# A first-layer token block moves to seven products, its weight values go through DRAM, and one block's token values change engine

## The chip, the cores and the metric

The kernel runs on one core of one Trainium2 chip, as one launch. The metric is the device time of a run in microseconds (us). Five engines work side by side, each through its own instructions in order: TensorE (PE in the profile), VectorE (DVE), ScalarE (ACT), GpSimd (POOL) and SyncE (SP), which here only issues DMA transfers.

## The reference

Clustered attention feeds two dense layers, all in float32. The change touches only the two layers and the last steps of attention beside which the first layer starts.

```python
attn_out = _attn_ref(q, k, v, centroids)              # 2 batches, 8 heads, 768 tokens, head size 64
x = attn_out.transpose(0, 2, 1, 3).reshape(1536, 512)
...
h = x @ w_in                                          # first layer: 512 -> 2048
x = (np.maximum(h, 0) + np.log1p(np.exp(-np.abs(h)))) @ w_out   # 2048 -> 512
...
h = x @ w_in2                                         # second layer, same sizes
out = (h * np.clip(h + 3.0, 0.0, 6.0) / 6.0) @ w_out2
```

The four weight matrices arrive as float64. The kernel reads them as pairs of 32-bit words and builds float32 values from the bits.

## The kernel before

**Steps.** The 1536 tokens are cut into three blocks of 512 (block 0, 1, 2), the 2048 hidden columns into 16 pieces of 128 (f = 0 to 15). One step n = (layer, block, f) forms the hidden values of one piece for one block (`phase_a`, 12 matmuls of 512 columns), passes them through the layer's function (`hid_scalar`, `hid_gate`, `hid_hi`, `hid_lo`), and adds their product with `w_out` to the block's four output banks y0 to y3 (`phase_b`, 12 matmuls of 512 columns; `back` issues them LAG = 2 steps later). There are 12 matmuls and not 4 because each float32 operand is kept as a rounded part and a rest (`xhi`/`xlo` for tokens, `pi`/`po` for weights, `ghi`/`glo` for hidden values) and three of the four partial products are computed. The first layer is n = 0 to 47, the second n = 48 to 95.

**Conversion.** In block 0 of the first layer the pieces of the weights are converted while they are used: piece f in step f - 2, both its `w_in` part (tiles `ri`, `pi`) and its `w_out` part (`ro`, `po`). `convert_abs` is a ScalarE copy (L123) into a tile `val`, `convert_bits` three VectorE operations on it (L131, L133, L137, in this order), `convert_parts` a ScalarE copy that rounds (L147), `convert_rest` a subtraction (L158, in this block on VectorE). The tiles `val` come from a pool of four buffers in the layers, two per step; in attention the pool has one. The copies for step n + 1 are made at the end of step n. Conversion of the second layer's pieces is spread over later steps.

**Fetching.** Pieces 7 to 15 of the first layer are fetched by 18 transfers of 512 KB (`fetch_w`, L103), which stand on SP's queue right behind the transfers of the last attention step (`row`, and `rsb`, which spreads the softmax sums). Transfers count their completion on eight semaphores in turn, DMAHW0 to DMAHW7, and one that is about to count on a semaphore first waits for the transfer that counted there before it.

**Pairs.** In the second layer, blocks 1 and 2 run two steps at a time by Strassen's scheme. The 2x2 cut is: two hidden pieces (f, f + 1), two halves of the 512 input columns, two halves of the block's tokens. Seven products (`product`, L1054, six matmuls of 256 columns each) take the place of eight. Four of them need sums of weights (`factor_totals` on VectorE, `factor_part` on ScalarE and GpSimd) and sums of tokens (`token_sums`), which stand in the columns of `xhi` and `xlo` that held the block before (`token_parts`). The sums of weights are made from the float32 values of `w_in`. So `keep_values` stores each second-layer `val` of `w_in` to DRAM when its third bit operation is done (L971), and `factor_fetch` brings it back (L980).

**Ends of blocks.** `finish_block` empties y0 to y3 when a block's last `phase_b` is done: ScalarE writes the rounded part into `xhi` (L922), VectorE the rest into `xlo` (L923). For block 2 ScalarE also copies each bank to a tile `tok` (L927), from which the token sums of the second layer's block 2 are made.

Of the kernel before, what the change touches and what calls it, by code (L numbers as in the profile page):

```python
# [22 lines left out]
def cluster_attention_then_two_mlps(  # L23
# [30 lines left out]
    def f32(ap):  # L54
        return ap.bitcast(F32)
# [114 lines left out]
    steps = [(l, tb, f) for l in range(2) for tb in range(NB) for f in range(NF)]  # L170
    ps_h = []
    hs = {}
    last_flip = []

# [12 lines left out]
    def attention():  # L187
        with ExitStack() as st, ExitStack() as st_ld, ExitStack() as st_ps:
# [514 lines left out]
            at(94, 2, convert_bits, *piece, 2)  # L703
            at(94, 3, convert_parts, *piece, False)
# [165 lines left out]
    spill = ctx.enter_context(tc.tile_pool(name="spill", bufs=1, space=bass.MemoryType.DRAM))  # L870
# [25 lines left out]
    def hidden(layer, h, paired=False):  # L896
        t = {"h": h, "layer": layer}
        t["ghi"] = tmp.tile([P, TB], F32R, tag="ghi", name="ghi")
        t["glo"] = tmp.tile([P, TB], F32R, tag="glo", name="glo")
        if layer == 1:  # L900
# [62 lines left out]
    fac, tok, part, kept = {}, {}, {}, {}  # L963
    A, Bp = slice(0, TB // 4), slice(TB // 4, TB // 2)
    near, far = slice(0, NC // 2), slice(NC // 2, NC)

    def keep_values(layer, f, nm):

        if layer == 1 and nm == "i":
            kept[f] = spill.tile([P, NC, P], F32, tag=f"v{f}", name=f"v{f}")  # L970
            nc.sync.dma_start(kept[f], pieces[layer, f, nm][1])  # L971

    def factor_fetch(n):

        layer, tb, f = steps[n]
        if tb == 1:
            fac[n] = []
            for e in range(2):
                v = wpools["val"].tile([P, NC, P], F32, tag="val", name="wv")
                nc.sync.dma_start(v, kept[f + e])  # L980
# [15 lines left out]
    def factor_part(n, e):  # L996
        if n in fac:
            w = part[n, e] = win.tile([P, 2, NC, P], F32R, tag=f"s{e}", name=f"s{e}")
            nc.scalar.activation(w[:, 0], fac[n][e], AF.Copy)
            nc.gpsimd.tensor_tensor(w[:, 1], fac[n][e], f32(w[:, 0]), ALU.subtract)  # L1000
            f = steps[n][2]
# [3 lines left out]
    def token_values(c):  # L1005
        cols = slice(TB, 2 * TB)
        x = tok[1, c] = win.tile([P, 2, TB], F32, tag=f"x{c}", name=f"x{c}")
        for e in range(2):
            k = c + 2 * e
            nc.gpsimd.tensor_tensor(x[:, e], f32(xhi[k][:, cols]), f32(xlo[k][:, cols]), ALU.add)  # L1010

    def token_sums(tb, c, step):
# [7 lines left out]
        nc.gpsimd.tensor_tensor(o, p, q, ALU.subtract)  # L1020
# [45 lines left out]
    with tc.manual_schedule():  # L1066
        gs, ysd = {}, {}
        late = None
# [27 lines left out]
        for n in range(first_pair):  # L1096
# [19 lines left out]
            if (NB - 1) * NF + LAG < n <= (NB - 1) * NF + LAG + 4:  # L1116
                k = n - (NB - 1) * NF - LAG - 1
                if k % 2 == 0:
                    token_values(k // 2)
                for m in range(k % 2 * 2, k % 2 * 2 + 2):  # L1120
                    token_sums(1, k // 2, m)
            k = n - NB * NF - LAG - 1
            if 0 <= k < 8:
                token_sums(2, k // 4, k % 4)
                if k % 4 == 3:
                    token_store(2, k // 4)
# [31 lines left out]
        order = [(first_pair - 2, None, None), (first_pair - 1, None, None)]  # L1158
        for n in range(first_pair, len(steps), 2):
            f = steps[n][2]  # L1160
            order += [(n, f == 0, False), (n + 1, False, f == NF - 2)]

        def backs():
            for what in order:
                yield from back(*what)

        chunks = backs()
        for n in range(first_pair, len(steps), 2):
            layer, tb, f = steps[n]
            more = n + 2 < len(steps)  # L1170
            change = f == NF - 2 and tb + 1 < NB
# [8 lines left out]
            if tb + 1 < NB and f == 6:  # L1180
# [39 lines left out]
        for _ in chunks:  # L1220
            pass
# [47 lines left out]
```

## Time and profile before

| | |
|---|---|
| median of 3 runs (lowest to highest) | 749.52 us (749.39 to 750.17) |
| the profiled execution, its own time | 749.33 us |
| its span in the profile | 747.6 us |
| granted TensorE clock over the span | 1.00 of full |
| TensorE / VectorE / ScalarE / GpSimd busy | 724.9 / 538.4 / 441.9 / 200.3 us |

The span runs from the first to the last recorded instruction. The difference to the execution's time lies around it. Attention fills the span up to about 249 us, the first layer from there to about 506 us (block 0 until about 338, block 1 until about 420), the second layer the rest. Times of single rows are starts, counted from the start of the span.

### The profile page before, as it was taken

What the parts mean: (1) busy time and instruction counts of PE and PEld (TensorE: products, weight loads), DVE (VectorE), ACT (ScalarE), POOL (GpSimd) and SP (SyncE); (2) the same over time, 40 slices, a digit from 0 to 9 for tenths busy, and PEclk for the clock granted to TensorE, in tenths of its full rate; (3) what the DMA queues carried; (4) which work ended last, traced back from release to release, by engine and by line L of the source; (5) the groups of instructions that cost most, each with busy time, mean ns of one, the idle gap of its engine ahead of it and who ended that gap; (6) DMA issues with size and microseconds to landing.
All of it is one profiled execution on the core that took longest, in us unless ns stands there. A gap on an engine that the chain in (4) does not pass through costs nothing.

```text
span 747.6 us, 11713 instructions
## 1 busy us (share of the span) xinstructions
PE 724.9 (97%) x4129; PEld 642.3 (86%) x4129; DVE 538.4 (72%) x932; ACT 441.9 (59%) x859; POOL 200.3 (27%) x267
## 2 busy tenths in 40 slices
PE   7999999999999899999999999998999999999997
PEld 6788899898888788788888888886888999999997
DVE  5999889889898999942111258887996888765553
ACT  6889889889998856632212346565565444533322
POOL 3667768767435000000000410003002422410000
PEclk9999999999999999999999999999999999999999
DMA  7656776666474490000000267771114364235311
GB/s 197 176 142 171 171 199 178 164 186 163 111 194 152 164 363 1 2 0 1 1 0 1 71 209 246 236 236 45 71 57 155 142 226 169 115 137 200 113 57 57
DMA packets 50410, 98.66 MB, mean 132 GB/s; under 512 B 5904, under 2 KB 26800, under 8 KB 50352
## 3 DMA queue, kind: packets, MB, share of 16 engines
q1 hardware_dynamic: 50208, 97.79, 42.4%
q8 instruction: 32, 0.52, 0.3%
q14 instruction: 26, 0.21, 0.1%
q10 hardware_dynamic: 144, 0.13, 0.1%
HBM read 59.93 MB, written 16.83 MB: 103 GB/s over the span
## 4 chain that ended last, share of the span: by engine, by line
PE 69%; DVE 18%; ACT 6%; issue 4%; DMA 1%; POOL 1%; SPq 0%; ACTq 0%; DVEq 0%; POOLq 0%
PE y L914 16%; PE h L183 15%; PE y L912 10%; PE h L1054 10%; PE t L452 6%; PE s L422 5%; PE pv L467 5%; DVE val L133 4%; DVE val L137 3%; DVE ptl L457 2%; DVE nm L430 2%; DVE val L131 2%; PE psm L322 2%; ACT pr L438 2%; ACT pth L456 2%
## 5 line engine op out<-in xcount | busy, mean ns | idle before, releaser
L183 PE MATMUL h<-xhi,pi 128*128 128x512 f32 x512 | 156.0, 382 | 3.6 <-DVE pi L158 2.5
L894 DVE TENSOR_TENSOR glo<-g,ghi 128x512 fp32r<-128x512 f32 x64 | 45.1, 705 | 105.9 <-ACT ghi L881 100.1
L914 PE MATMUL y<-po,ghi 128*128 128x512 f32 x384 | 114.8, 381 | 3.1 <-ACT x L927 3.1
L183 PEld LDWEIGHTS h<-xhi,pi 128*128 128x128 f32 x512 | 96.3, 189 | 22.1 <-DVE pi L158 7.9
L912 PE MATMUL y<-ghi,po 128*128 128x512 f32 x384 | 114.3, 379 | 0.1
L457 DVE TENSOR_TENSOR ptl<-t,pth 128x384 fp32r<-128x384 f32 x192 | 97.6, 548 | 20.7 <-ACT pth L456 20.4
L183 PE MATMUL h<-xlo,pi 128*128 128x512 f32 x256 | 97.0, 379 | 0.0
L456 ACT ACTIVATE pth<-t 128x384 fp32r<-128x384 f32 x192 | 86.2, 491 | 10.5 <-PE t L452 9.3
L430 DVE TENSOR_REDUCE nm<-s 128x1 f32<-128x768 f32 x96 | 90.5, 944 | 1.6 <-PE s L422 1.5
L452 PE MATMUL t<-ident,pr 128*128 128x128 f32 x576 | 86.7, 279 | 4.4 <-DVE ptl L457 4.1
L438 ACT ACTIVATE pr<-s,nm 128x768 f32<-128x768 f32 x96 | 86.8, 904 | 5.4 <-DVE nm L430 4.6
L422 PE MATMUL s<-K,Q 128*128 128x256 f32 (+1 forms) x384 | 85.9, 346 | 3.1 <-ACT pr L438 2.2
L880 ACT ACTIVATE g<-h 128x512 f32<-128x512 f32 x48 | 28.4, 591 | 91.8 <-PE h L183 91.7
L912 PEld LDWEIGHTS y<-ghi,po 128*128 128x128 f32 x384 | 72.5, 189 | 10.7 <-ACT xs L487 0.5
L452 PEld LDWEIGHTS t<-ident,pr 128*128 128x128 f32 x576 | 65.0, 141 | 18.7 <-DVE ptl L457 15.7
L1157 DVE TENSOR_TENSOR hp<-h,hp 128x256 f32<-128x256 f32 x112 | 45.9, 422 | 43.9 <-PE h L1054 41.6
L914 PEld LDWEIGHTS y<-po,ghi 128*128 128x128 f32 x384 | 67.5, 190 | 11.3 <-ACT x L927 4.7
L422 PEld LDWEIGHTS s<-K,Q 128*128 128x128 f32 x384 | 65.9, 190 | 10.0 <-ACT pr L438 3.5
L914 PE MATMUL y<-po,glo 128*128 128x512 f32 x192 | 72.9, 380 | 0.0
L912 PE MATMUL y<-glo,po 128*128 128x512 f32 x192 | 72.8, 379 | 0.0
L467 PE MATMUL pv<-pth,vs 128*128 128x384 f32 x192 | 63.2, 329 | 0.6 <-ACT xs L487 0.6
L467 PE MATMUL pv<-ptl,vs 128*128 128x384 f32 x192 | 62.5, 326 | 0.0
(152 smaller groups left out, 1317.8 us busy)
## 6 DMA issues: line engine op xcount, KB each, us to landing
ri<-in_moe_w_in SPq DMA_DIRECT2D x29, 512.0 KB, 6.9
ro<-in_moe_w_out SPq DMA_DIRECT2D x29, 512.0 KB, 3.4
k<-s SPq DMA_DIRECT2D x16, 512.0 KB, 2.8
s<-k SPq DMA_DIRECT2D x16, 512.0 KB, 3.6
K<-hik SPq DMA_DIRECT2D x31, 192.0 KB, 5.0
Q<-hiq SPq DMA_DIRECT2D x15, 384.0 KB, 3.9
v<-val SPq DMA_DIRECT2D x16, 256.0 KB, 2.2
wv<-v SPq DMA_DIRECT2D x16, 256.0 KB, 3.2
```

The lines of the kernel that those rows point to most:

```text
L183: nc.tensor.matmul(hs[n][:, :TB], w[:, c, :], turned(x[c][:, cols]), start=(c == 0 and i == 0), stop=(c == NC - 1 and i == 2))
L422: nc.tensor.matmul(ps[:, n0:n1], Q[i][:, u, j * P:(j + 1) * P], turned(K[i][:, u])[:, n0 // 2:n1 // 2], start=(u == 0), stop=(u == 1),)
L430: nc.vector.tensor_reduce(nm, st_s[t][:, :S], AX.X, ALU.max, negate=True)
L438: nc.scalar.activation(pr, st_s.pop(t)[:, :S], AF.Exp, bias=st_p[t], accum_out=sums_of[n][:, i, j:j + 1])
L452: nc.tensor.transpose(pt[:, c * P:(c + 1) * P], pr[:, kt * P:(kt + 1) * P], ident)
L456: last_flip[:] = [nc.scalar.activation(dh, src, AF.Copy)]
L457: nc.vector.tensor_tensor(dl, src, f32(dh), ALU.subtract)
L467: nc.tensor.matmul(st_v[h][:, :HALF], vs[:, kt, i, :], turned(st_t[h][u][:, kt, :]), start=(kt == 0 and u == 0), stop=(kt == NJ - 1 and u ...
L912: nc.tensor.matmul(y[:, :TB], w[:, e, :], turned(x), **fl)
L914: nc.tensor.matmul(y, x[:, e * P:(e + 1) * P], turned(w.rearrange("p c e -> p (c e)")), **fl)
L1054: nc.tensor.matmul(o, u[:, wc + r, :], turned(x[xc + r][:, cols])[:, half_], start=(r == 0 and i == 0), stop=(r == 1 and i == 2),)
L1157: add = lambda o, p, q: nc.vector.tensor_tensor(o, p, q, ALU.add)
```

## The change

Block 1 of the first layer runs f = 2 to 15 as seven pairs. f = 0 and 1 stay single steps, and so do blocks 0 and 2. For this

- `keep_values` now also stores the `w_in` values of f = 2 to 15 of the first layer to DRAM during block 0, 14 transfers of 256 KB on SP's queue, and they are fetched back during block 1;
- in steps 14 to 17 the token values, the token sums and their parts for block 1 are made (values on GpSimd, sums and rests on VectorE), and the parts overwrite block 0's columns of `xhi` and `xlo`, which are no longer read by then;
- `finish_block` keeps block 0's outputs whole in two tiles `tok`, by one ScalarE copy per bank and no VectorE operation; in step 32, behind block 1, `token_parts` splits them into `xhi` and `xlo`;
- the extra ScalarE copies at the end of block 2 are gone; GpSimd adds `xhi` and `xlo` later instead (`token_values`), in steps 51 to 58. The token values of the second layer's block 1 are made in steps 35 to 38, as before, in another order.

```diff
+    def keep_values(layer, f, nm):
+
+        if nm == "i":
+            kept[layer, f] = spill.tile([P, NC, P], F32, tag=f"v{f}", name=f"v{f}")
+            nc.sync.dma_start(kept[layer, f], pieces[layer, f, nm][1])
...
             at(94, 2, convert_bits, *piece, 2)
+            at(94, 2, keep_values, *piece)
...
             for e in range(NC):
                 y = in_order(ys[e][:, :TB])
+                if tb == 0:
+                    if e < 2:
+                        tok[tb, e] = win.tile([P, 2, TB], F32, tag=f"x{e}", name=f"x{e}")
+                    nc.scalar.activation(halved(tok[tb, e % 2][:, e // 2]), y, AF.Copy)
+                    continue
                 hi, lo = halved(xhi[e][:, cols]), halved(xlo[e][:, cols])
                 nc.scalar.activation(hi, y, AF.Copy)
                 nc.vector.tensor_tensor(lo, y, f32(hi), ALU.subtract)
-                if tb == NB - 1:
-                    if e < 2:
-                        tok[tb, e] = win.tile([P, 2, TB], F32, tag=f"s{e}", name=f"x{e}")
-                    nc.scalar.activation(halved(tok[tb, e % 2][:, e // 2]), y, AF.Copy)
...
+    pairs = [*range(NF + 2, 2 * NF, 2), *range(first_pair, len(steps), 2)]
...
+            for tb, tag, k in ((1, "x", 2 * early), (1, "x", 2 * early + 1), (2, "s", early - NF)):
+                if 0 <= k < 8:
+                    c = k // 4
+                    if k % 4 < 2:
+                        token_values(tb, c, k % 4, tag)
...
+            if n in (NF - 2, NF - 1):
+                for e in range(2):
+                    token_values(1, n - NF + 2, e, "x")
+            if n == NF - 1:
+                factor_fetch(pairs[0])
+            if n in (NF - 1, NF):
+                for k in range(4):
+                    token_sums(1, n - NF + 1, k, nc.vector)
+            if n == NF:
+                token_parts(1, 0, range(NC), nc.vector)
+            if n == NF + 1:
+                factor_totals(pairs[0])
+                factor_fetch(pairs[0] + 2)
+                for e in range(2):
+                    factor_part(pairs[0], e)
+            if n == 2 * NF:
+                token_parts(0, 0, range(NC), nc.vector)
...
+        while n < len(steps):
+            if n in pairs:
+                pair(n)
+                n += 2
+            else:
+                step(n)
+                n += 1
```

The order of the instructions, at the three places that matter below. First SP's queue at the end of attention, before the change: the last attention transfers, and behind them the 18 fetches `ri7` to `ro15`.

```order
L483 DMA xs1_3654<-xs0_3653 64x384 [waits DMAHW0_49,Activation_49,Pool_49]
L509 DMA row_3751<-rT_3749 12x128 [waits DMAHW1_49,Activation_49]
L516 DMA rsb_3753<-row_3751 64x768 [waits DMAHW5_49,DMAHW6_49,DMAHW1_49,Pool_49]
...
L103 DMA ri7_3807<-in_moe_w_in 128x4x256 [waits DMAHW4_49,PE_49]
L103 DMA ro7_3809<-in_moe_w_out 128x1024 [waits PE_49]
L103 DMA ri8_3811<-in_moe_w_in 128x4x256
...
L103 DMA ro15_3841<-in_moe_w_out 128x1024 [waits DMAHW5_49,Pool_49]
```

The same place after the change. `v2`, `v3` and so on are the stores of the values of f = 2, 3 and so on; each waits for VectorE.

```order
L492 DMA xs1_3656<-xs0_3655 64x384 [waits DMAHW0_49,Activation_49,Pool_49]
L182 DMA v2_3681<-val_3618 128x512 [waits DMAHW1_49,DVE_49]
L518 DMA row_3755<-rT_3753 12x128 [waits Activation_49]
L182 DMA v3_3863<-val_3852 128x512 [waits DMAHW3_49,DVE_49]
L525 DMA rsb_3757<-row_3755 64x768 [waits DMAHW5_49,DMAHW4_49,DMAHW6_49,DMAHW2_49,Pool_49]
...
L182 DMA v4_3900<-val_3872 128x512 [waits DVE_49]
L104 DMA ri7_3809<-in_moe_w_in 128x4x256 [waits DMAHW7_49,PE_49]
L104 DMA ro7_3811<-in_moe_w_out 128x1024 [waits DMAHW0_49,PE_49]
...
L104 DMA ro15_3843<-in_moe_w_out 128x1024 [waits DMAHW0_49,Pool_49]
L182 DMA v5_3953<-val_3909 128x512 [waits DMAHW1_49,DVE_49]
L182 DMA v6_4002<-val_3962 128x512 [waits DMAHW2_49,DVE_49]
```

Three stores now stand ahead of the first fetch, the third of them, `v4`, directly ahead of `ri7`. The next, `v5`, stands behind all 18 fetches. The store `v5` counts on DMAHW1.

Next ScalarE in step 4 of block 0, before the change: the second softplus operation of the step (`ghi`), the copies that open the conversion of piece 7, and the rounding copies of the pieces 6 and 7.

```order
L881 ACTIVATE ghi_3985<-h_3972 128x512
L123 ACTIVATE val_4001<-ri7_3807 128x512 [waits DMAHW4_49]
L123 ACTIVATE val_4005<-ro7_3809 128x512 [waits DMAHW5_49,Activation_49]
L147 ACTIVATE po6_4035<-val_3958 128x512 [waits DVE_49]
L147 ACTIVATE pi7_4041<-val_4001 128x512 [waits DVE_49,Activation_49]
```

The same place after the change.

```order
L890 ACTIVATE ghi_3993<-h_3980 128x512
L124 ACTIVATE val_4011<-ri7_3809 128x512 [waits DMAHW7_49,Activation_49]
L124 ACTIVATE val_4015<-ro7_3811 128x512 [waits DMAHW1_49,DMAHW0_49]
L148 ACTIVATE po6_4045<-val_3966 128x512 [waits DVE_49]
L148 ACTIVATE pi7_4053<-val_4011 128x512 [waits DVE_49,Activation_49]
```

The instructions are the same. The copy from `ro7` now waits for DMAHW1, the semaphore of `v5`: it writes the buffer that this store reads.

Last, ScalarE at the end of block 2, before the change: each bank is read twice, with a wait for VectorE ahead of the second read.

```order
L922 ACTIVATE xhi0_96<-y0_5100 128x512 [waits PE_49]
L927 ACTIVATE x0_5828<-y0_5100 128x512 [waits DVE_49]
L922 ACTIVATE xhi1_97<-y1_5101 128x512 [waits PE_49]
L927 ACTIVATE x1_5832<-y1_5101 128x512 [waits DVE_49]
L922 ACTIVATE xhi2_98<-y2_5102 128x512 [waits PE_49]
L927 ACTIVATE x0_5828<-y2_5102 128x512 [waits DVE_49]
L922 ACTIVATE xhi3_99<-y3_5103 128x512 [waits PE_49]
L927 ACTIVATE x1_5832<-y3_5103 128x512 [waits DVE_49]
```

And after the change, where four copies are left that wait for TensorE alone, and the next conversion follows.

```order
L936 ACTIVATE xhi0_96<-y0_5464 128x512 [waits PE_49]
L936 ACTIVATE xhi1_97<-y1_5465 128x512 [waits PE_49]
L936 ACTIVATE xhi2_98<-y2_5466 128x512 [waits PE_49]
L936 ACTIVATE xhi3_99<-y3_5467 128x512 [waits PE_49]
L148 ACTIVATE po8_6215<-val_6120 128x512 [waits DVE_49,Activation_49]
```

The four copies to `tok` are gone, and what stood between the four rounding copies with them.

## Rows read from the trace of the kernel before

**Rows 1.** The page: busy time of each engine over the span.
```profile
PE 724.9 (97%) x4129; PEld 642.3 (86%) x4129; DVE 538.4 (72%) x932; ACT 441.9 (59%) x859; POOL 200.3 (27%) x267
```

**Rows 2.** Chain of work that ended last, 225 to 350 us: by line, and one piece.
```profile
by line: DVE val L133 18.2%; issue 14.0%; DVE val L137 13.7%; PE h L183 12.8%; PE y L912 10.4%; DVE val L131 8.0%; DVE glo L894 3.7%; DVE pi L158 2.0%; ACT pth L456 1.7%; ACT val L123 1.7%; PE t L452 1.6%; ACT pr L438 1.6%; PE s L422 1.6%; 
...
322.45 2.64 PE h L183 x11
```

**Rows 3.** TensorE in order of time: starts of steps in block 0 and 1.
```profile
271.38 0.38 PE L183 MATMUL h<-xhi,pi 128*128 128x512 f32 x1
...
276.98 0.38 PE L183 MATMUL h<-xhi,pi 128*128 128x512 f32 x1
...
327.52 0.59 PE L183 MATMUL h<-xhi,pi 128*128 128x512 f32 x2
...
332.70 0.59 PE L183 MATMUL h<-xhi,pi 128*128 128x512 f32 x2
```

**Rows 4.** Busy time (and instructions) by engine in block 1, and in paired steps.
```profile
345.00:428.00 83.00, 83.00 (x386) 72.69 (x385) 13.52 (x20) 19.44 (x36) 6.91 (x7) 1.00 0.03 9
595.00:660.00 65.00, 65.00 (x433) 60.67 (x432) 51.53 (x96) 30.32 (x50) 20.15 (x16) 1.00 0.49 181
```

**Rows 5.** TensorE in order of time: where two pairs of the second layer begin.
```profile
580.49 0.38 PE L1054 MATMUL h<-xhi,pi 128*128 128x256 f32 x2
...
590.36 0.38 PE L1054 MATMUL h<-xhi,pi 128*128 128x256 f32 x2
```

**Rows 6.** TensorE in order of time: around the end of block 2.
```profile
506.01 0.38 PE L183 MATMUL h<-xlo,pi 128*128 128x512 f32 x1
...
512.96 0.59 PE L183 MATMUL h<-xhi,pi 128*128 128x512 f32 x2
```

**Rows 7.** ScalarE in order of time: ends of block 0 and of block 2.
```profile
336.46 2.22 ACT L922 ACTIVATE xhi<-y 128x512 fp32r<-128x512 f32 x4
...
506.02 0.60 ACT L927 ACTIVATE x<-y 128x512 f32<-128x512 f32 x1 [0.76 <-DVE xlo L923]
```

**Rows 8.** VectorE in order of time: conversion of weights in block 0.
```profile
239.60 0.69 DVE L137 SCALAR_TENSOR_TENSOR val<-ri,val 128x512 uint32<-128x512 uint32 x1
...
257.20 0.86 DVE L137 SCALAR_TENSOR_TENSOR val<-ri,val 128x512 uint32<-128x512 uint32 x1
...
274.26 0.68 DVE L158 TENSOR_TENSOR po<-val,po 128x512 fp32r<-128x512 f32 x1
```

**Rows 9.** ScalarE in order of time: three copies in conversions.
```profile
242.40 0.74 ACT L123 ACTIVATE val<-ro 128x512 f32<-128x512 f32 x1 [0.74 <-POOL pi L158]
...
272.31 0.85 ACT L123 ACTIVATE val<-ro 128x512 f32<-128x512 f32 x1
273.06 0.61 ACT L147 ACTIVATE po<-val 128x512 fp32r<-128x512 f32 x1
```

**Rows 10.** DMA issues on SP's queue in order of time.
```profile
250.37 1.10 SPq L516 DMA_DIRECT2D rsb<-row  x2
251.57 0.54 SPq L103 DMA_DIRECT2D ri<-in_moe_w_in  x1
...
269.38 2.26 SPq L103 DMA_DIRECT2D ro<-in_moe_w_out  x1
```

**Rows 11.** Waits of SP's queue: line, releaser, total, times, longest.
```profile
SPq L971 <- DVE val L131: 62.0, 15, 9.5
```

**Rows 12.** The issue of `ri15` at 268.84 us: size, us to landing.
```profile
ri<-in_moe_w_in SPq DMA_DIRECT2D x1, 512.0 KB, 9.5
```

**Rows 13.** The page: issues of the stores of values, size, us to landing.
```profile
v<-val SPq DMA_DIRECT2D x16, 256.0 KB, 2.2
```

**Rows 14.** Windows of 2 us while pieces are fetched; last column GB/s.
```profile
252.00:254.00 2.00, 2.00 (x11) 1.75 (x10) 2.00 (x4) 1.93 (x3) 0.00 (x0) 1.00 0.70 193
276.00:278.00 2.00, 1.81 (x9) 1.27 (x8) 1.97 (x4) 2.00 (x5) 0.00 (x0) 1.00 1.07 405
278.00:280.00 2.00, 2.00 (x11) 1.76 (x10) 1.97 (x5) 1.27 (x2) 0.00 (x0) 1.00 0.25 100
```

More of the change, by code (lines that the diff above doesn't have):

```diff
@@ L1 @@
+import itertools
 from contextlib import ExitStack
@@ L170, in cluster_attention_then_two_mlps @@
     steps = [(l, tb, f) for l in range(2) for tb in range(NB) for f in range(NF)]
+    spill = ctx.enter_context(tc.tile_pool(name="spill", bufs=1, space=bass.MemoryType.DRAM))
+    kept = {}
     ps_h = []
@@ L899, in hidden @@
         t["glo"] = tmp.tile([P, TB], F32R, tag="glo", name="glo")
-        if layer == 1:
+        if layer == 1 or paired:
             t["u"] = tmp.tile([P, TB], F32, tag="u", name="u", bufs=2)
@@ L962, in cluster_attention_then_two_mlps @@
     first_pair = NF * (NB + 1)
-    fac, tok, part, kept = {}, {}, {}, {}
+    pairs = [*range(NF + 2, 2 * NF, 2), *range(first_pair, len(steps), 2)]
+    fac, tok, part = {}, {}, {}
     A, Bp = slice(0, TB // 4), slice(TB // 4, TB // 2)
     near, far = slice(0, NC // 2), slice(NC // 2, NC)
[L967 to L971, printed above, removed]
     def factor_fetch(n):
@@ L979, in factor_fetch @@
                 v = wpools["val"].tile([P, NC, P], F32, tag="val", name="wv")
-                nc.sync.dma_start(v, kept[f + e])
+                nc.sync.dma_start(v, kept[layer, f + e])
                 fac[n].append(v)
@@ L1000, in factor_part, with token_values, token_sums @@
             nc.gpsimd.tensor_tensor(w[:, 1], fac[n][e], f32(w[:, 0]), ALU.subtract)
-            f = steps[n][2]
+            layer, _, f = steps[n]
+            if layer == 0:
+                return
             s = kept["s", f, e] = spill.tile([P, 2, NC, P], F32, tag=f"s{f}{e}", name=f"k{f}{e}")
             nc.sync.dma_start(s, f32(w))
[L1005 to L1012, printed above, removed]
+    def token_values(tb, c, e, tag):
+        cols = slice(tb * TB, (tb + 1) * TB)
+        if e == 0:
+            tok[tb, c] = win.tile([P, 2, TB], F32, tag=f"{tag}{c}", name=f"x{c}")
+        k = c + 2 * e
+        nc.gpsimd.tensor_tensor(tok[tb, c][:, e], f32(xhi[k][:, cols]), f32(xlo[k][:, cols]), ALU.add)
+    def token_sums(tb, c, step, engine=nc.gpsimd):
         x0, x1 = (halved(tok[tb, c][:, e]) for e in range(2))
@@ L1019, in token_sums @@
         )[step]
-        nc.gpsimd.tensor_tensor(o, p, q, ALU.subtract)
+        engine.tensor_tensor(o, p, q, ALU.subtract)
     def token_store(tb, c):
@@ L1067, in cluster_attention_then_two_mlps @@
         gs, ysd = {}, {}
-        late = None
+        late = cur = None
         pend = lambda n: {nm: (l, f, nm) for l, f in convert_at.get(n, ()) for nm in "io"}
@@ L1094, in back, with step @@
                 yield
-        for n in range(first_pair):
+        def step(n):
+            nonlocal cur, nxt, late
             cur, nxt = nxt, pend(n + 1)
@@ L1157, in cluster_attention_then_two_mlps, with pair @@
         add = lambda o, p, q: nc.vector.tensor_tensor(o, p, q, ALU.add)
[L1158 to L1168, printed above, removed]
+        def pair(n):
+            chunks = itertools.chain(back(n - 2), back(n - 1))
             layer, tb, f = steps[n]
-            more = n + 2 < len(steps)
-            change = f == NF - 2 and tb + 1 < NB
+            more = n + 2 in pairs
+            change = more and f == NF - 2
             p16, p25, p74 = (ps_h[0].tile([P, 512], F32, tag="h", name="h") for _ in range(3))
@@ L1179, in cluster_attention_then_two_mlps @@
                 factor_fetch(n + 2)
-            if tb + 1 < NB and f == 6:
+            if layer == 1 and tb == 1 and f == 6:
                 for c in range(2):
@@ L1219, in cluster_attention_then_two_mlps @@
                 next(chunks)
-        for _ in chunks:
-            pass
+        n = 0
+        while n < len(steps):
+            if n in pairs:
+                pair(n)
+                n += 2
+            else:
+                step(n)
+                n += 1
+        for n in range(len(steps) - LAG, len(steps)):
+            for _ in back(n):
+                pass
 def kernel(**inputs):
```

17 lines of the change are left out of this document (5 added, 12 removed).

## The prediction

> **What bounds the kernel now.** I read the busy times first. TensorE works 724.9 of 747.6 us [rows 1], so over the whole kernel only matmuls saved or TensorE's gaps closed can pay. An average hides stages with other limits, so the chain of waits comes next, for the stretch in which the change begins. There, in block 0 of the first layer, the chain does not run on TensorE: it is VectorE's conversion of the weights (L133, L137, L131), until 322.45 us, where a long piece of TensorE takes over [rows 2]. TensorE's own rows say the same. A step takes 276.98 - 271.38 = 5.60 us in block 0 and 332.70 - 327.52 = 5.18 us in block 1 [rows 3]. So each step of block 0 loses 0.42 us waiting for converted weights, and nothing that delays the conversion is hidden there. From block 1 on TensorE is the limit: it is busy for 83.00 of 83 us while VectorE, ScalarE and GpSimd work 13.52, 19.44 and 6.91 us [rows 4]. In the second layer's pairs it is busy 65.00 of 65 us, although VectorE works 51.53 us of them [rows 4].
>
> **What the pairs save.** A pair takes 590.36 - 580.49 = 9.87 us [rows 5], two single steps 2 x 5.18 = 10.36 us [rows 3]. That is 0.49 us for each of seven pairs, **-3.4 us**. The first layer's pairs have fewer VectorE and ScalarE operations around the same matmuls than the second layer's, which TensorE does not wait for; so I take all of it. The other end is 0: every pair loses its gain to a late operand.
>
> **What the end of block 2 saves.** The last matmul of the step ahead starts at 506.01 [rows 6]. With a pitch of 5.18 / 24 = 0.216 us, its 12 successors would be through, and the next step begin, at 506.01 + 13 x 0.216 = 508.82. It begins at 512.96 [rows 6], so 4.1 us are lost. ScalarE's copy of y0 to `tok` explains them: it waited 0.76 us for VectorE's rest and then held the bank for 0.60 us [rows 7], and so on four times in a row. Without these copies the four rounding copies run in 2.22 us, as at the end of block 0 [rows 7]. VectorE's rest of y0 was done at 506.02, where the copy to `tok` starts. The rests of y1 to y3 then follow at most 0.7 us apart (a subtraction of this size takes 0.68 [rows 8]), while TensorE asks for a bank every 0.65 us, first at 506.23. It then finds each one free: **-4.1 us**, with 3.5 as the low end.
>
> **What is costed at nothing.** GpSimd's value additions and the sums move to steps 14 to 17, 35 to 38 and 51 to 58, where GpSimd has room [rows 4]. Block 0's ending needs fewer operations than before. The token parts, sums and first totals of steps 14 to 17 are about 20 VectorE operations of at most 0.9 us in four steps of 5.18, after the conversion is over. TensorE's work of steps 15 to 17 hides them; if that cover fails, the first pair starts late, and I hold up to 2 us for it. Transfers back from DRAM in block 1 meet idle queues (9 GB/s [rows 4]).
>
> **The stores: what they wait for, and who waits for them.** This is the part of the change that I price highest. Three stores now stand ahead of the fetches on SP's queue, and SP works in order: it has stood up to 9.5 us in front of a store of this kind, waiting for VectorE [rows 11].
>
> The store `v2` reads the only `val` buffer of attention. Its values are done at 239.60 + 0.69 = 240.29 [rows 8], a store needs 2.2 us to land [rows 13], so the buffer is free at 242.5 and not at 242.40, where ScalarE's next copy into it starts, after waiting for GpSimd [rows 9]. **+0.2 us** (0 to 1).
>
> The store `v4` needs VectorE's third operation on piece 4, which ends at 257.20 + 0.86 = 258.06 [rows 8]. Directly behind it stands the fetch of piece 7, which now starts at 251.57 [rows 10]. After the change it starts at about 258.06 + 0.54 = 258.6 (one issue, as long as that of `ri7`), 7.0 us later. The fetches still arrive in time: piece 7 is first read at 272.
>
> But `v5` stands behind all 18 of them. Before the change the last bytes came at 278.5 (the window from 278 moved only 100 GB/s, a quarter of the full rate [rows 14]), 26.9 us after the first issue. `rsb` shared the slow beginning (193 GB/s [rows 14]) and is now out of the way, worth about 1 us. At the full 405 GB/s throughout, 18 x 0.524 MB would take 23.3 us, the short end. I take 26: the fetches end at 258.6 + 26 = 284.6. The store's own 0.26 MB take 0.65 us. Then some fixed time passes: `ri15`, issued at 268.84, landed 9.5 us later at 278.3 [rows 12], 1.1 us after its bytes, which end one piece (1.3 us) before the last. So `v5` lands at 284.6 + 0.65 + 1.1 = **286.4** (283.1 to 287.6).
>
> What waits for that is ScalarE's copy from `ro7`: it writes the buffer that `v5` reads. Before, it started at 272.31 [rows 9]; it will be 14.1 us late. Queued behind it on ScalarE are the rounding copies of pieces 6 and 7 and the softplus of the next step; VectorE waits for the first of these, and TensorE for the weights. There is a little slack: the rounding copy `po` ended at 273.06 + 0.61 = 273.67 [rows 9], and VectorE took its result only at 274.26 [rows 8], 0.6 us later. So everything from step 5 on shifts by 14.1 - 0.6 = **+13.5 us** (10.2 to 14.7). It happens once: `v6` lands 0.65 us behind `v5`, and the later stores find an empty queue, as the second layer's do.
>
> **Sum.** -3.4 - 4.1 + 0.2 + 13.5 = +6.2 us. The profiled execution took 749.33 us and stands 0.19 us under the median of the runs, too little to matter: **755.5 us**.
>
> **Rivals.** (a) The store does not queue behind the bytes of the fetches. It is issued behind the last fetch, at 269.38 + 2.26 + 7.0 = 278.6 [rows 10], and lands 2.2 us later at 280.8. The shift is then 280.8 - 272.31 - 0.6 = 7.9 us, and the sum +0.6: 749.9 us. Against it speaks the landing of `ri15`: 9.5 us, when a piece by itself needs 1.3 us of transfer, is a time spent in line [rows 12]. The Trainium skill (DMA: Bandwidth & Descriptors, Queues, rings and completion order) says that descriptors of one ring are consumed in order, though completions need not be. By the first half of that rule 755.5 stands, by the second a landing somewhat ahead of the last fetch, with the sum between 749.9 and 755.5; the trace agrees with the first half, at 9.5 us.
>
> (b) Faster: no stall. It would be so if `v5` landed before 272.9, that is if SP were not held in order by a store that waits. Then only -3.4 - 4.1 + 0.2 remain: 742.0 us. For it speaks that the second layer's 16 stores run on the same queue among fetches and TensorE keeps its pace; but there one store follows each pair of fetches, not 18 fetches. Against it speaks the 9.5 us wait [rows 11]. The change decides at a landing of `v5` at 272.9 + 7.3 = 280.2: earlier is faster, later slower.
>
> (c) Slower still: TensorE, idle for some 13 us in step 7, comes back at its lower clock. The granted clock is 1.00 in all windows shown [rows 4, 14], so no row has a price. If a whole step ran at half speed, TensorE would be 5.18 us late; the eight steps from 7 to 15 give back 0.42 us each, 3.4 in all, since VectorE runs its own course. That leaves +1.8: 757.3 us. The Trainium skill (TensorE: Matmul & The Clock Gate, Why this matters for your kernels) warns that a long idle gap between bursts of matmuls brings the clock back to half. No run here has such a gap; by that rule the loss is at least begun, and what counts is whether the steps up to 15 absorb it.
>
> **How the numbers follow.** The forecast has a chance of 0.62, (c) 0.14, (a) 0.10, (b) 0.14. The forecast by itself reaches from 751.5 to 758, by the bounds of the landing, of the first pair and of `v2`. With (c), and with (a) at its lower edge, 749.9 to 758.5 leaves out (b) and little else. A measurement here can tell about 0.2%, 1.5 us, from no change. (a) counts as no change, (b) as faster: faster 0.14, same 0.10, slower 0.76.
>
> **What would show it.** In the profile after, ScalarE has one long idle stretch of 13 to 15 us at about 273 us, ended by a DMA store of `val`, with VectorE and TensorE idle at the same time; SP issues `ri7` at about 258 and the store `v5` at about 278. Pairs in block 1 are 9.87 us apart, and no TensorE wait stands at the end of block 2. I would be wrong if ScalarE's copy from `ro7` starts near 272 us, if it starts near 281 (a), or if the pairs of block 1 are longer than two steps of 5.18 us. A granted clock under 1.00 behind the idle stretch, with TensorE still the last to be ready at step 15, would be (c).

## The result, and the profile after

The changed kernel takes 760.03 us (median of 4 runs, 758.73 to 760.09), the kernel before beside it 749.85 us: a ratio of 1.0125, with a 95% interval of 1.0108 to 1.0142. So it is slower, as forecast, but 1.5 us beyond the range. The profiled execution took 760.09 us, its span is 758.3 us, 10.7 us longer than before. TensorE works no longer than before [rows 1]; the rest is waiting:

```profile
PE 724.7 (96%) x4255; PEld 647.0 (85%) x4255; DVE 581.1 (77%) x1021; ACT 461.0 (61%) x884; POOL 231.1 (30%) x289
```

**The stall stands where it was forecast.** SP's queue in order of time (start, duration, line): the store `v4`, the fetch `ri7` directly behind it, the last fetch, and the stores `v5` and `v6`. Then ScalarE's waits (releaser, total, times, longest) and the windows around them (columns as in [rows 4]).

```profile
259.81 0.33 SPq L182 DMA_DIRECT2D v<-val  x1
260.24 0.39 SPq L104 DMA_DIRECT2D ri<-in_moe_w_in  x1
...
277.28 1.62 SPq L104 DMA_DIRECT2D ro<-in_moe_w_out  x1
279.02 0.83 SPq L182 DMA_DIRECT2D v<-val  x2
```

```profile
ACT val L124 <- DMA v<-val: 12.7, 1, 12.7
```

```profile
275.00:280.00 5.00, 4.85 (x23) 3.91 (x21) 1.99 (x4) 0.05 (x1) 0.00 (x0) 1.00 1.06 401
280.00:285.00 5.00, 0.00 (x0) 0.00 (x0) 0.00 (x0) 0.00 (x0) 0.00 (x0) 0.70 1.06 399
285.00:290.00 5.00, 0.00 (x0) 0.00 (x0) 1.03 (x2) 1.18 (x2) 0.00 (x0) 0.50 0.47 185
290.00:295.00 5.00, 3.81 (x8) 2.76 (x9) 4.93 (x10) 3.25 (x6) 0.00 (x0) 0.50 0.14 52
```

From 280 to 285 us all five columns stand at 0.00 while the DMA engines move 399 GB/s: the store's bytes wait behind those of 18 fetches. ScalarE's copy from `ro7` starts at 287.76 instead of 272.31 [rows 9], TensorE's next step at 291.04. The granted clock falls from 1.00 to 0.50, the lower of its two levels, 1.2 GHz.

**The pairs and the end of block 2 do what was said.** Block 1 begins 14.48 us later than before [rows 3] (TensorE):

```profile
342.00 0.38 PE L192 MATMUL h<-xhi,pi 128*128 128x512 f32 x1
```

Its pairs begin at 352.36 and 362.23, 9.87 us apart, all seven alike, and the bank waits at the end of block 2 are gone. But right behind it something new stands. GpSimd, VectorE and TensorE in order of time:

```profile
517.08 2.51 POOL L1017 TENSOR_TENSOR x<-xhi,xlo 128x512 f32<-128x512 f32 x2 [73.23 <-DVE xlo L937]
519.55 4.53 POOL L1027 TENSOR_TENSOR x<-x 128x256 f32<-128x256 f32 x4
524.05 3.23 POOL L1017 TENSOR_TENSOR x<-xhi,xlo 128x512 f32<-128x512 f32 x2
527.24 4.65 POOL L1027 TENSOR_TENSOR x<-x 128x256 f32<-128x256 f32 x4
```

```profile
521.06 1.20 DVE L159 TENSOR_TENSOR po<-val,po 128x512 fp32r<-128x512 f32 x1
...
523.43 0.93 DVE L132 TENSOR_SCALAR val<-val 128x512 uint32<-128x512 uint32 x1
524.40 1.75 DVE L134 SCALAR_TENSOR_TENSOR val<-ro,val 128x512 uint32<-128x512 uint32 x1
526.08 1.75 DVE L159 TENSOR_TENSOR pi<-val,pi 128x512 fp32r<-128x512 f32 x1
527.75 0.67 DVE L896 SCALAR_TENSOR_TENSOR g<-u,h 128x512 f32<-128x512 f32 x1
528.35 0.68 DVE L138 SCALAR_TENSOR_TENSOR val<-ro,val 128x512 uint32<-128x512 uint32 x1
```

```profile
529.14 0.70 PE L923 MATMUL y<-po,ghi 128*128 128x512 f32 x2 [1.33 <-ACT ghi L900]
530.21 0.48 PE L923 MATMUL y<-po,glo 128*128 128x512 f32 x1 [0.38 <-DVE glo L903]
```

GpSimd runs for 15 us without a pause, VectorE's `po<-val,po` takes 1.20 us and `pi<-val,pi` 1.75, where `po<-val,po` took 0.68 [rows 8], and TensorE waits for `ghi` and `glo`. VectorE had no room for that. One step just ahead, in the changed kernel and then in the kernel before (columns as in [rows 4]; VectorE is the third):

```profile
509.51:514.69 5.18, 5.18 (x25) 4.54 (x24) 5.08 (x9) 2.71 (x5) 0.00 (x0) 1.00 0.64 194
...
498.46:503.64 5.18, 5.18 (x26) 4.54 (x25) 5.08 (x9) 2.71 (x5) 0.00 (x0) 1.00 0.60 182
```

To compare runs I use the loss over steps 50 to 57: the time between the starts of steps 50 and 58, less 8 x 5.18 us. It is 4.33 us before and 3.93 after. So of the 4.1 us saved, 0.4 are left.

Not all of the 3.93 us is waiting. Behind the two waits of TensorE the granted clock falls to 0.50 from 532 to 534 us, which it does not at this place in the kernel before. Changed kernel:

```profile
532.00:537.00 5.00, 5.00 (x19) 4.12 (x18) 4.31 (x8) 2.87 (x5) 0.00 (x0) 0.74 0.14 52
```

In runs 1 and 2 below, which have the same work there, the clock stays at 1.00 behind the same two waits (1.33 and 0.38 us), and the loss is 3.22 and 3.14 us. So some 0.7 to 0.8 us of the 3.93 go with the clock.

**Attention ends later.** Two of GpSimd's additions for block 1 run inside attention already, since nothing holds them back:

```profile
235.26 1.01 POOL L531 TENSOR_TENSOR xs<-xs,rsb 128x384 f32<-128x384 f32 x1
236.22 1.47 POOL L1017 TENSOR_TENSOR x<-xhi,xlo 128x512 f32<-128x512 f32 x1
...
238.56 1.26 POOL L1017 TENSOR_TENSOR x<-xhi,xlo 128x512 f32<-128x512 f32 x1
```

```profile
239.95 1.43 DVE L138 SCALAR_TENSOR_TENSOR val<-ri,val 128x512 uint32<-128x512 uint32 x1
...
249.23 0.69 DVE L903 TENSOR_TENSOR glo<-g,ghi 128x512 fp32r<-128x512 f32 x1
```

L138 takes 1.43 us instead of 0.69 [rows 8], and `glo` of the first step starts at 249.23 instead of 247.49.

| term | predicted | measured, from step starts |
|---|---|---|
| seven pairs | -3.4 | -3.43 |
| end of block 2, with the steps behind it | -4.1 | -0.40 |
| end of attention | +0.2 | +1.74 |
| stall at `ro7` | +13.5 | +12.74 (block 1 begins 342.00 - 327.52 = 14.48 later, less 1.74) |
| sum | +6.2 | +10.65 (span: +10.7) |

### The profile page after: what moved, and what is told of

Same layout as the page of the kernel before. It is cut to its first block, busy times and chain, and to the rows that moved or that the text cites. A ratio compares the mean times of both kernels' runs of the same rounds, so it can differ in the third digit from the quotient of the medians.

```text
span 758.3 us, 12214 instructions
## 1 busy us (share of the span) xinstructions
PE 724.7 (96%) x4255; PEld 647.0 (85%) x4255; DVE 581.1 (77%) x1021; ACT 461.0 (61%) x884; POOL 231.1 (30%) x289
## 4 chain that ended last, share of the span: by engine, by line
PE 72%; DVE 14%; ACT 7%; issue 3%; DMA 3%; SPq 1%; POOL 0%; ACTq 0%; DVEq 0%
PE y L923 16%; PE h L1061 14%; PE y L921 12%; PE h L192 12%; PE t L461 6%; PE pv L476 5%; PE s L431 5%; DVE val L134 3%; DVE ptl L466 2%; DVE nm L439 2%; ACT pr L447 2%; DVE val L138 1%; ACT pth L465 1%; PE psm L331 1%; DVE val L132 1%
## 5 line engine op out<-in xcount | busy, mean ns | idle before, releaser
L192 PE MATMUL h<-xhi,pi 128*128 128x512 f32 x400 | 124.2, 389 | 15.0 <-ACT pi L148 11.4
L1182 DVE TENSOR_TENSOR hp<-h,hp 128x256 f32<-128x256 f32 x161 | 66.0, 422 | 62.2 <-PE h L1061 59.0
L1005 POOL TENSOR_TENSOR s<-wv,s 128x512 fp32r<-128x512 f32 x30 | 38.4, 1300 | 228.6 <-ACT s L1004 221.3
L192 PEld LDWEIGHTS h<-xhi,pi 128*128 128x128 f32 x400 | 76.7, 193 | 30.1 <-ACT pi L148 12.2
L921 PEld LDWEIGHTS y<-ghi,po 128*128 128x128 f32 x384 | 70.5, 190 | 9.8 <-ACT xs L496 1.0
L192 PE MATMUL h<-xlo,pi 128*128 128x512 f32 x200 | 76.6, 383 | 0.0
L1061 PE MATMUL h<-xhi,s 128*128 128x256 f32 x368 | 63.9, 275 | 0.0
L903 DVE TENSOR_TENSOR glo<-g,ghi 128x512 fp32r<-128x512 f32 x50 | 36.6, 731 | 34.6 <-ACT ghi L890 28.7
```

Of the source, the lines that this page charges most:

```text
L192: nc.tensor.matmul(hs[n][:, :TB], w[:, c, :], turned(x[c][:, cols]), start=(c == 0 and i == 0), stop=(c == NC - 1 and i == 2))
L921: nc.tensor.matmul(y[:, :TB], w[:, e, :], turned(x), **fl)
L1061: nc.tensor.matmul(o, u[:, wc + r, :], turned(x[xc + r][:, cols])[:, half_], start=(r == 0 and i == 0), stop=(r == 1 and i == 2),)
L1182: add = lambda o, p, q: nc.vector.tensor_tensor(o, p, q, ALU.add)
```

## The experiments

Ratios are to the kernel before in the same session (medians of 750.3 to 751.3 us). Rows come from one execution of each run, which lies up to 4.1 us from the run's median (run 5: 758.16 against 762.27 us).

**1. The stores on another queue.**

```diff
-            nc.sync.dma_start(kept[layer, f], pieces[layer, f, nm][1])
+            (nc.sync if layer else nc.gpsimd).dma_start(kept[layer, f], pieces[layer, f, nm][1])
```

> The changed kernel, with the first layer's 14 stores of values issued by GpSimd instead of SyncE, so that none stands in SP's queue among the fetches. Theory (ScalarE's copy from ro7 waits 12.7 us for the store v5, because v5 stands in SP's queue behind the fetches): ri7 is issued near 252 us again, the copy from ro7 starts within 3 us of 272.3 + 2.7, the step that began at 342.0 begins near 330, and the time falls by 11 to 13 us, to about 748 us. Rival (the bytes of the fetches and the store share the DMA engines, whichever queue issues the store): the store still lands late, the copy still waits 6 us or more, and the time stays above 754 us.

Measured: 0.9984 (0.9965 to 1.0004). The stall is gone: between 272 and 286 us TensorE works 13.67 of 14. So it hung on SP's queue, not on the sharing of the DMA engines. Block 1 begins at 332.91, and not near 330. Two things are in this. The additions now run at steps 14 and 15, because GpSimd's queue stands in front of the stores; they give the cleanest look at their price.

```profile
322.87 0.68 DVE L159 TENSOR_TENSOR po<-val,po 128x512 fp32r<-128x512 f32 x1
...
325.40 1.73 DVE L159 TENSOR_TENSOR pi<-val,pi 128x512 fp32r<-128x512 f32 x1
327.04 1.89 DVE L138 SCALAR_TENSOR_TENSOR val<-ro,val 128x512 uint32<-128x512 uint32 x1
328.87 1.73 DVE L903 TENSOR_TENSOR glo<-g,ghi 128x512 fp32r<-128x512 f32 x1
```

```profile
325.24 6.49 POOL L1017 TENSOR_TENSOR x<-xhi,xlo 128x512 f32<-128x512 f32 x4
```

The same operation takes 0.68 us just ahead of GpSimd's stretch and 1.73 us in it; that step of TensorE took 7.32 us instead of some 5.6, a price of 1.7 us. The other thing lies earlier: TensorE's step 15 already begins 3.7 us later than before. Attention ran late in this execution, and `v2` costs something here. GpSimd stands 1.29 us in front of it, waiting for VectorE, and ScalarE's next copy into that `val` waits for it to land:

```profile
245.59 0.89 ACT L124 ACTIVATE val<-ro 128x512 f32<-128x512 f32 x1 [1.52 <-DMA v<-val]
```

**2. Block 1's values on VectorE.**

```diff
-                    token_values(1, n - NF + 2, e, "x")
+                    token_values(1, n - NF + 2, e, "x", nc.vector)
```

> The changed kernel, with the four value additions of block 1's first half (steps 14 and 15) on VectorE, so that GpSimd does not run three of them early, in and behind attention, at 236.2, 238.6 and 260.3 us. Theory (these additions slow VectorE and hold up GpSimd's own queue there, 1.74 us at the end of attention and 0.95 us at the step behind it): VectorE's glo at 249.23 comes back to about 247.5, L134 at 261.09 takes 0.7 instead of 1.65 us, and the time falls by 2 to 2.7 us, to about 757.4 us. Rival (the delay at the end of attention comes from the store v2, which holds the only val buffer): the time stays within 0.6 us of the changed kernel's.

Measured: 1.0124 (1.0095 to 1.0153), no gain: by the time alone the rival. The rows say more. Attention itself ran late in this execution (its second `xs` at 237.05 instead of 235.26), and the additions on VectorE made the first pair 10.80 us long instead of 9.87. Measured from that `xs` to `glo`, which leaves out how early an execution came to this point, the five runs with the additions in attention (the changed kernel, 3, 5, 6 and 9) take 13.45 to 14.39 us; the kernel before takes 11.40, and the six other runs with the store `v2` on SP's queue (2, 4, 7, 8, 10 and 11) 11.12 to 11.88. So the additions cost about 2 us there, and `v2` on SP's queue nothing that can be told from scatter. Run 1, with no addition there and `v2` on GpSimd's queue, takes 14.13. That moving them pays in time this run does not show.

**3. ScalarE's copies to `tok` at the end of block 2 put back, GpSimd's additions there left out.**

```diff
                 nc.vector.tensor_tensor(lo, y, f32(hi), ALU.subtract)
+                if tb == NB - 1:
+                    if e < 2:
+                        tok[tb, e] = win.tile([P, 2, TB], F32, tag=f"s{e}", name=f"x{e}")
+                    nc.scalar.activation(halved(tok[tb, e % 2][:, e // 2]), y, AF.Copy)
...
-                        token_values(tb, c, k % 4, tag)
+                        if tb == 1:
+                            token_values(tb, c, k % 4, tag)
```

> The changed kernel, with its part at the end of block 2 undone: ScalarE copies y to tok there again, as before, and GpSimd makes only the sums in the steps behind it. Theory (the 4.1 us saved at the end of block 2 are lost again within two steps, because GpSimd's 8 extra value additions and its sums slow VectorE's work there to about half its pace): the loss of 4.1 us at the end of block 2 is back, the waits of TensorE at 529 to 531 us and the dip of the clock are gone, and the time is within 0.8 us of the changed kernel's, 759.5 to 761. Rival (the 3.9 us behind the end of block 2 have another cause, such as the steps' own order): the time rises by about 4 us, to 764.

Measured: 1.0143 (1.0113 to 1.0172). By time it can't be told from the changed kernel. The loss over steps 50 to 57 is 5.73 us against 3.93: 1.8 us, between the two theories. With the copies TensorE waits four times again and comes out 4.8 us late; the sums (still GpSimd's) run for 6.69 us from 521.57, mostly behind the last of these waits at 523.33, and TensorE waits for none of what they slow. Here the clock fell behind the waits, which it had not in the kernel before (last section).

**4. The kernel before, and nothing but the stores.** They are written and never read.

```diff
+            at(94, 2, keep_values, *piece)
...
-        if layer == 1 and nm == "i":
+        if nm == "i":
```

> The kernel before, with nothing of the change but the first layer's 14 stores of values on SyncE's queue (they are written and not read). Theory (the stall behind the store v5 alone costs 12 us in the end, and the clock's fall behind it costs nothing, since VectorE bounds the steps that follow): the time is 749.9 + 12 = about 762 us, between 761 and 763.5, and the end of attention is as before, VectorE's glo within 0.4 us of 247.49. Rival 1 (the store v2 explains the delay of 1.74 us at the end of attention): glo at about 249.2, and about 763.5 us. Rival 2 (as predicted, 13.5 us for the stall alone): 763.4 us with glo at 247.5. Rival 3 (the stall needs the rest of the change): within 3 us of the kernel before.

Measured: 1.016 (1.0131 to 1.0188), 12 us. ScalarE waits for the store as in the changed kernel:

```profile
ACT val L123 <- DMA v<-val: 14.0, 1, 14.0
```

Block 1 begins at 339.62, 12.10 us later than before; `glo` starts at 246.59, 0.9 us earlier than before, so the stall itself is 13.0 us. The stores alone make the stall, so rival 3 falls, and rival 1 with it: `v2` delays nothing here. Theory and rival 2 differ only in the price of the stall, 12 or 13.5 us; the time fits both, and the 13.0 us of the rows lie between.

**5. Block 2 ends with copies to `tok` alone, and `xhi`, `xlo` are made from `tok`.** GpSimd makes the 8 sums and no values.

```diff
-                if tb == 0:
+                if tb != 1:
...
+            if tb == 2:
+                token_parts(2, 2, range(NC), nc.vector)
```

> The changed kernel with another end of block 2: ScalarE copies y to tok alone, as at the end of block 0, and xhi and xlo are made from tok behind it, so the banks are freed as fast, VectorE has as many operations as before, and GpSimd makes only the 8 sums and not the 4 value additions. Theory (the 3.1 to 3.9 us lost behind the end of block 2 in the changed kernel come from GpSimd's 15 us of unbroken work, which makes VectorE's operations there up to twice as long): the end of block 2 stays without a wait, at most 1 us is lost in the two steps behind it, and the time falls by 2 to 3.5 us against the changed kernel, to a ratio of 1.008 to 1.010. Rival (VectorE's four rests and the conversions are simply too much for those two steps, whatever GpSimd does): the loss of 3 us or more stays, and the ratio stays at 1.012.

Measured: 1.0135 (1.0103 to 1.0167); the loss over steps 50 to 57 is 3.45 us. My expectation missed: without the additions the loss stays (with them it was 3.22 and 3.14 us in runs 1 and 2, where the clock did not fall either). But GpSimd still worked 8.7 us on end:

```profile
517.69 8.68 POOL L1029 TENSOR_TENSOR x<-x 128x256 f32<-128x256 f32 x8 [75.30 <-DVE xlo L1045]
```

```profile
521.34 1.19 DVE L134 SCALAR_TENSOR_TENSOR val<-ri,val 128x512 uint32<-128x512 uint32 x1
522.46 1.21 DVE L159 TENSOR_TENSOR po<-val,po 128x512 fp32r<-128x512 f32 x1
523.60 1.31 DVE L138 SCALAR_TENSOR_TENSOR val<-ri,val 128x512 uint32<-128x512 uint32 x1
```

The four rests, which now read `tok`, take 3.57 us instead of 2.48. So the sums suffice, or VectorE alone is too slow; run 9 parts these two.

**6. The copies put back, and the additions kept too** (run 3 without the line that leaves them out).

> The changed kernel, with ScalarE's copies of y to tok at the end of block 2 put back, and GpSimd's value additions kept as well (they write the same values again). Against the run that put the copies back and took the additions out, GpSimd has 4 additions more and nothing else changes. Theory (GpSimd's additions lengthen VectorE's operations): 4.3 to 5.7 us are lost at the end of block 2, and 2 us or more in the steps behind it, so that the time is 2 to 3.5 us above that run, a ratio of 1.017 to 1.019. Rival (the additions cost nothing, and the loss in the changed kernel comes from the missing pause of TensorE): within 1 us of that run, 1.0143.

Measured: 1.0157 (1.0129 to 1.0185), against 1.0143 for run 3. That is the rival's number, though the interval reaches into the theory's. The rows decide: the loss is 6.16 us against 5.73. VectorE's operations were as long as 1.78 us, but TensorE came 4.8 us late out of its waits and had nothing to wait for in the two steps behind them. The waits that the change removes had given VectorE the time that GpSimd's work cost it.

**7. As run 4, without the store `v4`.**

```diff
-        if nm == "i":
+        if nm == "i" and (layer, f) != (0, 4):
```

> The kernel before with the first layer's stores of values on SyncE's queue, all but v4, the one that stands directly ahead of the fetches of pieces 7 to 15. Theory (the copy from ro7 is released 27.5 to 27.9 us after the issue of ri7, and the store v4 had held ri7 back by 6 to 7 us): ri7 is issued near 251.5 us again, the copy starts near 279.2, 6.4 us later than in the kernel before, and the time is 755 to 757.5 us, a ratio of 1.007 to 1.010. Rival (v4's place makes no difference, since v5 waits for the bytes of the fetches, which end when they end): the copy starts at 285 us or later and the ratio is 1.014 to 1.017.

Measured: 1.0086 (1.0055 to 1.0117). SP's queue and ScalarE's wait:

```profile
251.45 0.58 SPq L103 DMA_DIRECT2D ri<-in_moe_w_in  x1
...
271.93 0.80 SPq L181 DMA_DIRECT2D v<-val  x2
```

```profile
ACT val L123 <- DMA v<-val: 8.3, 1, 8.3
```

`ri7` goes out at 251.45, the copy starts at 280.22. So of the 12 us, a little under half are `v4` holding up the fetches, the rest is `v5` standing behind them. From the issue of `ri7` to the copy it is 27.5 to 27.9 us in the changed kernel and in runs 2 to 4, and 28.8 here.

**8. Four mends together.** Stores from `v4` on by GpSimd; run 2's values; run 5's end of block 2; and the first pair's factor parts behind the gate of step 17.

```diff
+            (nc.sync if layer or f < 4 else nc.gpsimd).dma_start(kept[layer, f], pieces[layer, f, nm][1])
...
-                for e in range(2):
-                    factor_part(pairs[0], e)
...
                 hid_lo(t)
+            if n == NF + 1:
+                for e in range(2):
+                    factor_part(pairs[0], e)
```

> The changed kernel with four mends: the first layer's stores from the fifth piece on are issued by GpSimd (those of the two pieces before them stay on SyncE's queue); the values of block 1's first half are added by VectorE; block 2 ends with ScalarE's copies to tok alone, with xhi and xlo made from tok; and the first pair's factor parts come behind the gate of step 17 instead of ahead of it. Theory (only the pairs, -3.4, and the end of block 2, -4.1, are left, less up to 1 us behind block 2 and 0.5 at the first pair): 742 to 744.5 us, a ratio of 0.990 to 0.993, faster than both. Rival (GpSimd's issuing of stores, at 0.54 us each, delays its own subtractions in the conversion, or the first pair stays late): 746 us or more, a ratio above 0.995.

Measured: 0.9943 (0.9923 to 0.9963), faster than both kernels, but by less than expected: behind block 2 it loses 3.42 us, as run 5 does.

**9. Run 5, with the 8 sums by VectorE in steps 60 and 61.** GpSimd does nothing behind block 2.

```diff
+            if n in (first_pair - 4, first_pair - 3):
+                c = n - first_pair + 4
+                for k in range(4):
+                    token_sums(2, c, k, nc.vector)
+                token_store(2, c)
```

> The run that ended block 2 with copies to tok alone, with one thing changed: the 8 sums of block 2's token values, which GpSimd made in one unbroken stretch of some 9 us behind the end of block 2, are made by VectorE in steps 60 and 61, when the conversions are over. So GpSimd works at nothing from 437 to 590 us, and VectorE's operations behind the end of block 2 stay what they were. Theory (GpSimd's work beside VectorE's lengthens VectorE's operations, which are the limit there, at 5.1 of 5.18 us): VectorE's L132, L134, L159 and L138 take 0.42, 0.84, 0.68 and 0.83 us again, the 3.4 us lost behind the end of block 2 in that run fall to 0.5 or less, and the time is about 3 us under it, 755.5 to 757.5 us, a ratio of 1.007 to 1.010. Rival (the loss comes of VectorE's four rests on top of the conversions, without any help of GpSimd): at least 2.5 us are still lost there, and the ratio stays above 1.011.

Measured: 1.0157 (1.0142 to 1.0171), so the time expected was missed. The question is settled all the same. The four rests take 2.50 us. The same three operations as under 5, and the four steps from 50 on:

```profile
522.22 0.85 DVE L134 SCALAR_TENSOR_TENSOR val<-ri,val 128x512 uint32<-128x512 uint32 x1
522.96 0.71 DVE L159 TENSOR_TENSOR po<-val,po 128x512 fp32r<-128x512 f32 x1
523.56 0.85 DVE L138 SCALAR_TENSOR_TENSOR val<-ri,val 128x512 uint32<-128x512 uint32 x1
```

```profile
515.75:536.47 20.72, 20.72 (x97) 18.14 (x96) 17.25 (x28) 13.85 (x24) 0.00 (x0) 1.00 0.20 70
```

The loss over steps 50 to 57 is 0.00 us. VectorE alone is fast enough; GpSimd's work beside it was the loss. But the second layer's first pair now takes from 588.27 to 602.02, 13.75 us instead of 9.87: what was won is given back.

**10. Run 8 with the same late sums.**

> The kernel with the four mends, with the same one thing changed: block 2's 8 sums by VectorE in steps 60 and 61. Theory: its 3.4 us lost behind the end of block 2 go, 742.5 to 744 us, a ratio of 0.989 to 0.991. Rival (VectorE alone is too slow there): the ratio stays at 0.994. Another (the sums in steps 60 and 61 make the first pair of the second layer late): the gain behind block 2 shows in the steps and is given back at the first pair, ratio 0.992 to 0.995.

Measured: 0.9945 (0.9925 to 0.9965): no loss behind block 2, and a first pair of 14.22 us, as its third theory said. SP's queue and VectorE name the cause:

```profile
560.07 4.02 SPq L1033 DMA_DIRECT2D kx<-x  x2
564.26 2.08 SPq L987 DMA_DIRECT2D wv<-v  x4
```

```profile
568.61 0.42 DVE L998 TENSOR_TENSOR wv<-wv 128x256 f32<-128x256 f32 x1 [2.92 <-DMA wv<-v]
```

The second store waits for its sums, and the fetch of the pair's factors stands behind it: `v4` once more.

**11. Those two stores by GpSimd.**

```diff
-        nc.sync.dma_start(kept["x", tb, c], tok[tb, c])
+        nc.gpsimd.dma_start(kept["x", tb, c], tok[tb, c])
```

> The run before this one, with one thing changed: GpSimd issues the two stores of block 2's token values, instead of SyncE. In that run SyncE's queue stood in front of these stores, which wait for the sums, while the fetch of the first pair's factors (L987) stood behind them; the factors came at 568.6 us, VectorE waited 2.92 us for them, and the second layer's first pair took 14.2 us instead of 9.87. Theory (a store that waits at the head of SyncE's queue holds up the fetches behind it, the same mechanism as at v4 and v5): the fetch is issued 2 us earlier or more, the first pair takes at most 10.5 us, and the time falls by 3.5 to 4.4 us, to 741 to 742.5 us, a ratio of 0.987 to 0.990. Rival (the pair is late because the parts s wait for the memory of the token values that are stored, whichever queue stores them): the first pair stays above 13 us and the ratio at 0.994.

Measured: 741.74 us, 0.988 (0.9857 to 0.9904), the fastest of all. The fetch goes out 8.5 us earlier, and the first pair lasts from 574.00 to 584.14:

```profile
555.74 4.42 SPq L987 DMA_DIRECT2D wv<-v  x4
```

## Why the prediction was wrong in size

- **The stall: right** in place, cause and price: +13.5 predicted, 12.7 to 13.0 found (changed kernel, run 4). From the issue of `ri7` to the copy I had 286.4 - 258.6 = 27.8 us; it was 27.5 to 27.9. In the changed kernel the copy came 15.45 - 1.74 = 13.7 us late instead of 14.1, and 1.0 us of that was absorbed instead of 0.6. The bounds of the landing, 283.1 and 287.6, don't follow from the working shown: 23.3 and 26.9 us in place of 26 give 283.7 and 287.3. Runs 1, 4 and 7 show both halves of it, the fetches behind `v4` and `v5` behind the fetches. Rivals (a) and (b) are out.
- **Rival (c)** came true as a fact and cost nothing. The clock fell to 0.50, but from 298.83 to 319.55 us TensorE's steps follow at 5.18 us, faster than the 5.60 us of block 0 before [rows 3], and from there on at 5.6 again, waiting for VectorE as before: it had caught up before block 1.
- **The pairs: right**, 9.87 us each. The 2 us held for the first pair were not needed in the changed kernel; runs 1 and 2 used 1.05 and 0.93 of them.
- **The step that failed is "What is costed at nothing".** It set GpSimd's additions and sums to zero because GpSimd has room where they go. What had no room was VectorE, and [rows 4], which the step leaned on, has no window behind block 2: there VectorE works 5.08 of 5.18 us, before the change too. Its operations take up to 2.6 times as long while GpSimd works (0.68 to 1.75 us in the changed kernel; runs 5 and 9 show them with and without it). Where VectorE has room, that costs nothing: in steps 34 and 35 of the changed kernel, beside the same GpSimd operations, VectorE works 2.63 and 0.74 us, and both steps take 5.18. In the kernel before, GpSimd's sums slowed VectorE behind block 2 as well, and ran mostly behind TensorE's four waits, the last of which ended at 512.21 us:

```profile
510.45 6.89 POOL L1020 TENSOR_TENSOR x<-x 128x256 f32<-128x256 f32 x7 [3.02 <-ACT x L927]
...
513.47 1.17 DVE L158 TENSOR_TENSOR po<-val,po 128x512 fp32r<-128x512 f32 x1
```

  But TensorE came out of these waits 4.1 us late and found its operands ready (run 6 shows that such a delay hides even more of GpSimd's work). The change takes the delay away, and the 4.1 us shrink to 0.40; of the missing 3.7 us some 0.7 to 0.8 go with the fall of the clock, the rest with GpSimd's work, as run 9 shows, where the loss is 0.00 us.
- **The +0.2 of `v2`** was the wrong cause for a delay that exists: on SP's queue `v2` has no visible price (run 4), while GpSimd's additions for block 1, run early inside attention, cost about 2 us there (run 2), of which 1.74 show in the start of `glo`.

These two account for 3.7 + 1.5 us; the stall was 0.8 less than said, which leaves the 4.4 us by which the sum was too low.

The Trainium skill (SBUF — State Buffer, Who interferes with whom) states that a VectorE instruction with two inputs in SBUF contends with a GpSimd instruction that reads SBUF. The traces agree for most such operations: 0.68 became 1.73 us in run 1. Not for each: L138 at 528.35 us took 0.68 beside GpSimd's sums in the changed kernel. By that rule, had I weighed it, GpSimd's moved work would have had a price wherever VectorE has no room.

## What to carry to other kernels

An idle engine is no free place for work until it is known which engine its work slows; look for the stretch where that second engine is the limit. When a wait of the bounding engine is removed, list which engines used the delay to catch up, since what slows them becomes visible next. A store that waits for a computation doesn't belong on the queue that issues the next fetches: taken off SP's queue twice, it gave back 10.6 us (run 1 against the changed kernel, by the ratios) and 4.1 (run 11 against run 10, at the first pair). The queue that takes it over stands in front of it in turn, as GpSimd's did in run 1.

## What the runs showed of the hardware, unexpected

- Not all of VectorE's work is slowed beside GpSimd: L896, whose second operand comes from PSUM, took 0.67 us in the midst of GpSimd's stretch, while L159 took 1.75. Nor is each operation with two operands in SBUF slowed: L138 right behind L896 took 0.68, and L903 in steps 34 and 35, beside the same GpSimd operations, 0.76 and 0.74 instead of 0.69. The one-operand L132 went from 0.42 to 0.93. What decides how much an operation is slowed these runs leave open.
- The clock's fall does not follow from the kernel's waits alone. At the end of block 2, TensorE stands four times, three times for 0.93 us, in the kernel before and in run 4 alike. Before (and in run 7) the clock stays at 1.00 there, with a loss of 4.33 us (4.32 in run 7); in run 4 (and in 3 and 6) it falls, and the loss is 5.84 (5.73 and 6.16). A window of the kernel before, and two of run 4:

```profile
511.00:513.00 2.00, 1.07 (x6) 0.72 (x5) 1.97 (x3) 1.11 (x2) 1.84 (x4) 1.00 0.03 8
```

```profile
524.00:526.00 2.00, 1.68 (x5) 1.45 (x6) 1.97 (x3) 0.78 (x2) 1.92 (x3) 0.72 0.00 0
526.00:528.00 2.00, 2.00 (x6) 1.55 (x6) 2.00 (x3) 0.13 (x1) 1.84 (x3) 0.50 0.00 0
```

Why it falls in some executions and not in others these runs leave open.
